# Block 0's second layer as seven products, output weights loaded ahead of batch 1, batch 2 in chunks turned by DMA

## The chip, the cores and the metric

The kernel runs on one core of a Trainium2 chip. A core has TensorE (PE; its weight loads are listed apart as PEld), VectorE (DVE), ScalarE (ACT), GpSimd (POOL), and SyncE (SP), which here does nothing but issue DMAs; 16 DMA engines move the data between HBM and the on-chip SBUF. PE writes its results into PSUM, eight banks of 128 partitions by 2 KB. The metric is the device time of one execution in microseconds (us), as a median of several.

## The reference

A retention layer without softmax over 8 batches of 8 heads, 576 tokens and 64 dimensions, and behind it two dense layers with a tanh GELU over all 4608 tokens:

```python
scores = scale * np.matmul(q, k.transpose(0, 1, 3, 2))
Dmat = np.where(rel >= 0, gamma[:, None, None] ** rel[None, :, :], 0.0)
attn = np.matmul(scores * Dmat[None, :, :, :], v)
x = np.ascontiguousarray(attn.transpose(0, 2, 1, 3)).reshape(B * S, H * D)   # 4608 x 512
h = x @ w_in                                                                 # 512 x 2048
g = 0.5 * h * (1.0 + np.tanh(c * (h + 0.044715 * h * h * h)))
return g @ w_out                                                             # 2048 x 512
```

All inputs and the output are float32. The decay factors over into a factor for each query row and one for each key row, so that only a triangular mask is left within a chunk of 128 tokens, and a running state of 64 x 64 for each head carries the past from chunk to chunk.

## The kernel before

**Blocks.** The dense layers run in nine blocks `t` of 512 tokens (`TB`). Blocks 0 to 7 hold the first 512 tokens of batch 0 to 7, block 8 the last 64 tokens (the tails) of all eight. The attention of batch `b = t + 1` is woven into block `t`, so block `t + 1` finds its input `xT`. A block's first layer is 16 column groups of `w_in` (`up`, L466, 4 matmuls of 512 columns each; `up_half`, L482, two groups for 256 tokens at a time in blocks 0 and 1), each followed by a GELU on ACT into `gT`. The last two blocks run part of the first layer as Strassen-like products.

**Second layer.** Blocks 1 to 8 run it as seven products in place of eight (`prod`, L651, a variant of Strassen's method with halves of the tokens, of the 2048 inner columns and of the 512 output columns). Each product `m` has two token halves `u` of 8 matmuls with 256 columns. It needs four sums of activations (`act_sums`, L637, DVE, into `gs`, one of them in place) and four of weights (`weight_sums`, L626, DVE, into `wt`); `after` (L673) collects the products on DVE and ACT into an output tile `ost` and stores it. Block 0 instead multiplies plainly: `down_mm` (L605), 64 matmuls of 512 columns over 16 rows-of-128 of `w_out` in the order `FO`, the first 12 for two pairs of token tiles, then the 4 late ones; `store_pair` (L610) copies and stores.

**Loads.** All of q, k, v and the weights go through 16 slots of 256 KB (`ld`), and every load is issued by SP from one list `seq` (L124), in order; a slot comes free when its cast to float16 is issued, and `pump` (L136) then issues the next load. Before: batch 0, `w_in`, 12 rows of `w_out`, half of batch 1, 4 rows of `w_out`, the rest of batch 1, batch 2, batch 3, the tails of batches 0 and 1 (`load_tails`, L81, own tiles `lt`), batch 4 and so on. In `load` (L91) batches below `NPE` (3) come in a pair layout, two neighbouring tokens to a partition, in runs of 512 bytes; later batches in 128-token chunks, in runs of 256 bytes.

**Attention.** In the pair layout keys and queries are cast and scaled on POOL or DVE (`cast`, L247), turned by PE (`turn`, L277, 8 transposes of 128 x 128, then one copy of 128 x 1024 on ACT) and used by `score2`, `masks2`, `state2`, `av2`. From batch `NPE` on they are turned by two DMA transposes on SP's queue (`turn_dma`, L296; its third, `ett`, turns the tails) and used by `score`, `masks`, `state`, `av`. `scan` (DVE) and `spread` (ACT) move the state on, `past` multiplies by it, `put` (ACT) writes `xT`.

**Order.** All is written by hand: `at(t, u, f)` puts work after step `u` of block `t`, negative steps lying in block 0's first layer. Engines run their own instructions in this order. For batch 3 and later the casts stand in block `b - 2` from step 16 on (L945 to L957): there the list of loads is put on hold, POOL waits on a small `gate` copy for the block's last activation sums, the transposes follow the last cast, and `resume` lets the loads go on at step 29, so that the transposes stand ahead of them in SP's queue. Loads already issued at that time, up to 16 slots, stand ahead of the transposes. The scores of batch `t + 1` come at steps 9 and 19 of block `t`, values at 15 and 25.

Of the kernel before, what the change touches and what calls it, by code (L numbers as in the profile page):

```python
# [20 lines left out]
def kernel(  # L21
# [9 lines left out]
    nc = tc.nc  # L31
# [9 lines left out]
    NH = NF // 2  # L41
    W = NC * 512
    NB = W // 128
    NPE = 3
    LD = 16
    TB = 512
    NI = TB // 128
# [13 lines left out]
    def bank(name, dt=F32):  # L61
        n = spare.popleft()
        t = ps.tile([128, 512 if dt == F32 else 1024], dt, tag=f"p{n}", name=name, bufs=1)
        home[id(t)] = (n, t)
        return t
# [53 lines left out]
    def body(b):  # L119
        if b < NPE:  # L120
            return [("b", b, key, 2 * g + y) for g in range(2) for key in "qkv" for y in range(2)]
        return [("b", b, key, c) for c in range(NC) for key in "kqv"]

    seq = body(0) + [("i", g, ct) for g in range(4) for ct in range(4)]  # L124
    FO = [f + g for f in (0, 4) for g in (0, 1, 2, 3, 8, 9, 10, 11)]
    LATE = 12
    seq += [("o", f) for f in FO[:LATE]]
    TP = {2: 0, 4: 2, 6: 4, 7: 6}
    seq += body(1)[:6] + [("o", f) for f in FO[LATE:]] + body(1)[6:]
    for b in range(1, B):  # L130
        seq += body(b) if b > 1 else []
        if b - 1 in TP:
            seq.append(("t", TP[b - 1]))
    q_ld = {"next": 0, "free": LD, "hold": False}

    def pump(freed=0):  # L136
        q_ld["free"] += freed
        while q_ld["next"] < len(seq) and not q_ld["hold"]:
            s = seq[q_ld["next"]]
            if s[0] != "t":  # L140
                if q_ld["free"] == 0:
                    return
                q_ld["free"] -= 1
            q_ld["next"] += 1
            {"b": load, "i": load_w_in, "o": load_w_out, "t": load_tails}[s[0]](*s[1:])
# [456 lines left out]
    def ost():  # L602
        return sb.tile([128, 2, DM], F32, tag="ost", name="ost", bufs=2)

    def down_mm(t, i, f):  # L605
        if f == FO[0]:
            op[i] = bank("op")
        nc.tensor.matmul(op[i], gT[t][:, f, i], w_out_sb[:, f, :], start=(f == FO[0]), stop=(f == FO[-1]))

    def store_pair(t, i0, eng):  # L610
        o = ost()
        for n in range(2):
            x = op.pop(i0 + n)
            eng[n](out=o[:, n], in_=x)
            drop(x)
        r0 = TB * t + 128 * i0
        nc.sync.dma_start(out=out[r0 : r0 + 256, :].rearrange("(n p) d -> p n d", n=2), in_=o)

    HD = DM // 2
    wt = {n: const.tile([128, NH, HD], F16, name="wt" + n) for n in "1234"}
    W11, W12 = w_out_sb[:, 0:NH, 0:HD], w_out_sb[:, 0:NH, HD:DM]
# [24 lines left out]
        if 1 in parts:  # L648
            nc.vector.tensor_tensor(out=s["4"], in0=a12, in1=s["2"], op=ALU.subtract)  # L649

    def prod(t, m, u):  # L651
        g = gT[t].rearrange("p f (u i) n -> p f u i n", i=2)
        lhs = {
            1: lambda f: g[:, f, u, 0], 2: lambda f: g[:, NH + f, u, 0], 3: lambda f: gs[t]["4"][:, f, u],
            4: lambda f: g[:, NH + f, u, 1], 5: lambda f: gs[t]["1"][:, f, u], 6: lambda f: gs[t]["2"][:, f, u],
            7: lambda f: g[:, f, u, 1],
        }[m]
        rhs = {1: W11, 2: W21, 3: W22, 4: wt["4"], 5: wt["1"], 6: wt["2"], 7: wt["3"]}[m]
        tag = {1: "A", 2: "A", 3: "C", 4: "D" if t in WIN else "B", 5: "C", 6: "B", 7: "B"}[m]
        if t in WIN and m == 3:  # L660
            tag = "EF"[u if t == NTB - 1 else 0]
        new = tag not in op
        if new:
            op[tag] = bank("op" + tag)
        for f in range(NH):
            nc.tensor.matmul(  # L666
                op[tag][:, HD * u : HD * u + HD], lhs(f), rhs[:, f],
                start=(new and f == 0), stop=(f == NH - 1), skip_group_check=True,
            )
# [3 lines left out]
    def after(t, m, u):  # L673
# [15 lines left out]
        def end(o, i, v, d=slice(0, DM)):  # L689
            b = 4 * v + 2 * i  # L690
            for h, e in enumerate((nc.sync, nc.scalar)):
                r0 = S * (b + h) + M0
                e.dma_start(out=out[r0 : r0 + TL, d], in_=o[TL * h : TL * h + TL, d])
        if m == 1:
            keep["s1"] = sb.tile([128, 2, HD], F32, tag="k1", name="k1", bufs=1)
            nc.scalar.copy(out=keep["s1"], in_=pr("A"))  # L696
# [39 lines left out]
    def cast_w(kind, *i):  # L736
        src = w_raw.pop((kind,) + i)
        if kind == "i":
            g, ct = i
            dst = w_in_sb[:, ct, 512 * g : 512 * g + 512]  # L740
        else:
            dst = w_out_sb[:, i[0], :]
        eng = WENG[kind][CP[kind] % len(WENG[kind])] if CP[kind] < LATE or kind == "i" else nc.gpsimd.tensor_copy
        CP[kind] += 1
        eng(out=dst, in_=src)  # L745
        pump(1)

    WENG = {
        "i": (nc.gpsimd.tensor_copy,),
        "o": (nc.gpsimd.tensor_copy, nc.vector.tensor_copy),  # L750
    }

    def cc(b, key, c, eng):
        cast(b, key, c, eng)
# [45 lines left out]
    for x in range(2):  # L800
        masks2(0, 1, x)
        if x == 0:
            later(0, 2)
    for g in range(4):
        for ct in range(4):
            cast_w("i", g, ct)
    up_half(0, 0, 0)
# [24 lines left out]


    at(0, -12, lambda: [V.memset(x, 0.0) for x in (tbd[1][:, 1:], *tbt[1:])])
    for n, f in enumerate(FO):
        at(0, -5 + n // 4 if n < LATE else 6, lambda f=f: cast_w("o", f))
        if 8 <= n < LATE:
            at(0, -5 + n // 4, lambda n=n: weight_sums(0, [n - 8], V))

    def group(b, g, turns, s, o, own=True, ahead=(), apart=0, late=None):  # L840
        for w, key in zip(turns, "qk"):
# [26 lines left out]
        if own:  # L868
            at(*(late or (o[0], o[1] + 1)), lambda: spread(b, 2 * g + 1, A.copy))

    def casts2(b, g, kq, v, e):
        at(*kq, lambda: [cc(b, key, 2 * g + y, P) for key in "qk" for y in range(2)])
        at(*v, lambda: [cc(b, "v", 2 * g + y, e) for y in range(2)])

    at(0, -1, lambda: (new_casts(1), new_turned(1)))
    casts2(1, 0, (0, 2), (0, 18), A)
    group(1, 0, ((0, 13), (0, 17)), (0, 20), (0, 29), apart=4, late=(1, 1))
    casts2(1, 1, (0, 14), (0, 15), P)
    group(1, 1, ((0, 31), (1, 0)), (1, 1), (1, 5), late=(1, 6))
    at(1, 0, lambda: (new_casts(2), new_turned(2)))  # L880
    casts2(2, 0, (1, 0), (1, 0), P)
    group(2, 0, ((1, 4), (1, 6)), (1, 10), (1, 15), ahead=((2, 1),))
    casts2(2, 1, (1, 4), (1, 4), P)
    at(1, 9, lambda: weight_sums(4, (1, 2), V))
    at(1, 12, lambda: weight_sums(4, (0, 3), V))
    at(1, 16, lambda: later(2, 2))
    at(1, 23, lambda: later(2, 3))
    group(2, 1, ((1, 9), (1, 12)), (1, 20), (1, 26), own=False)
    at(1, 14, chunk_masks)

    at(6, 0, lambda: load_tails(TP[7]))
    at(6, 18, lambda: cast_tails(TP[7]))
# [30 lines left out]
        for w in work:  # L923
            put(*w)

    nb = NPE
    at(1, 26, lambda: state(nb, 0, 1))
    for c in range(2):
        at(2, c, lambda c=c: later(nb, c))
    for t in range(2, B):  # L930
        b, tl = t + 1, TP.get(t)
        s0, o0, s1, o1 = 9, 15, 19, 25
        at(t, s0, lambda t=t, tl=tl: scores(t, 0, tl))
        at(t, o0, lambda t=t, b=b, tl=tl: outs(t, 0, tl, (b, 2, 3) if t < B - 1 else None))
        if b == B:
            continue
        at(t, s1, lambda t=t, b=b: scores(t, 2))
        at(t, o0 + 1, lambda b=b: later(b, 2))
        at(t, o1, lambda t=t, nb=b + 1: outs(t, 2, None, (nb, 0, 1) if nb < B else None))
        at(t, o1 + 1, lambda b=b: later(b, 3))  # L940
        if b + 1 < B:
            for c in range(2):
                at(t + 1, c, lambda c=c, nb=b + 1: later(nb, c))

    for b in range(NPE, B):  # L945
        ent = [(key, c) for c in range(NC) for key in "kqv"]
        eng = {"k": P, "q": P, "v": P if b == NPE else A}
        t0, ut = b - 2, [16, 16, 17, 18, 18, 19, 20, 20, 21, 22, 22, 23]
        if b == NPE:
            ut = [16, 16, 17, 19, 19, 20, 22, 22, 23, 25, 25, 26]  # L950
        at(t0, ut[0], lambda b=b: (new_casts(b), new_turned(b)))
        at(t0, ut[0], lambda: q_ld.update(hold=True))
        at(t0, ut[0], lambda t=t0: nc.gpsimd.tensor_copy(out=gate, in_=gs[t]["4"][:, NH - 1, 1, 0:1]))  # L953
        for u, (key, c) in zip(ut, ent):
            at(t0, u, lambda b=b, key=key, c=c, e=eng[key]: cc(b, key, c, e))
        at(t0, ut[-1] + 1, lambda b=b: turn_dma(b, TP.get(b - 1)))
        at(t0, 29, resume)  # L957

    order = [(u, g) for u, g in ((0, 0), (0, 1), (1, 0), (1, 1), (0, 2), (1, 2), (0, 3), (1, 3))]
    for n, (u, f) in enumerate([(u, f) for u, g in order for f in (4 * g, 4 * g + 2)]):  # L960
        if n > 1:
            up_half(0, u, f)
# [2 lines left out]
    for t in range(NTB):  # L965
        steps = []
        if t == 0:
            for i0, fs in ((0, FO[:LATE]), (2, FO[:LATE]), (0, FO[LATE:]), (2, FO[LATE:])):
                for f in fs:
                    steps.append(lambda f=f, i0=i0: [down_mm(0, i0 + n, f) for n in range(2)] and None)  # L970
                if fs[-1] == FO[-1]:
                    steps.append(lambda i0=i0: store_pair(0, i0, (V.tensor_copy if i0 else A.copy, V.tensor_copy)))
        else:
            for u in range(2 if t == 1 else 0):
                for f in (0, NH, 2, NH + 2, 4, NH + 4, 6, NH + 6):
# [81 lines left out]
```

## Time and profile before

| | before |
|---|---|
| time, median of 3 runs | 296.76 us (296.52 to 296.77) |
| profiled execution: time | 296.39 us |
| profiled execution: span, first to last instruction | 294.7 us |
| PE busy | 282.2 us, 96% of the span |
| DVE, ACT, POOL busy | 191.7, 168.4, 100.2 us |
| bytes read from HBM, written | 36.70 MB, 9.44 MB |
| DMA packets under 512 B, of all | 101632 of 129058 |
| PE at work on block 0's second layer, first and last matmul | 33.6 to 51.9 us |
| block 1, first and last matmul | 51.9 to 87.1 us |
| block 2's first matmul | 87.1 us |

The profiler draws one execution. The page has a row for each engine in 40 slices of the span (a digit is the busy share in tenths), groups of instructions by line of the kernel, and waits: the idle time of an engine just before an instruction, with what ended it. A matmul's own duration overlaps its neighbours, so a stream is priced by the distance between starts. A DMA has a time of issue on SP's queue and a time to landing. A busy DMA row says that packets were under way in all 16 engines; how much they moved is in the GB/s row.

### The profile page before, as it was taken

How to read it: one execution, taken by the hardware profiler on the slowest of the kernel's cores; microseconds unless marked ns; L12 is line 12 of the kernel's file. 1: busy time of each engine (PE TensorE's matmuls, PEld its weight loads, DVE VectorE, ACT ScalarE, POOL GpSimd, SP SyncE). 2: the span in 40 equal slices, each digit the busy share in tenths (PEclk: the TensorE clock that was granted, in tenths of full speed). 3: DMA queues.
4: the chain of work that ended last, by engine and by line, in shares of the span. 5: the costliest groups of instructions: out<-in, count | busy, mean ns of one | idle time of the engine just before them, and what ended most of it. 6: DMA issues, size and time to landing. Idle time of an engine off the chain costs nothing. (4 is left out here: it accounts for less than half of the span.)

```text
span 294.7 us, 7531 instructions
## 1 busy us (share of the span) xinstructions
PE 282.2 (96%) x3100; PEld 204.3 (69%) x3100; DVE 191.7 (65%) x396; ACT 168.4 (57%) x313; POOL 100.2 (34%) x133
## 2 busy tenths in 40 slices
PE   6779999999999999999999999999999999999993
PEld 2458745888884588448844885478547887887782
DVE  6790606789754873477448654855488968974863
ACT  5377443998239663866386736664666258507800
POOL 4587487960880082007700640059030000000000
PEclk9999999999999999999999999999999999999998
DMA  7999999999969998999899949944941030003013
GB/s 202 307 357 372 341 317 292 280 280 211 194 165 232 216 225 169 261 214 194 103 271 221 169 88 273 211 109 76 263 93 38 0 145 1 2 20 125 1 38 107
DMA packets 129058, 52.92 MB, mean 180 GB/s; under 512 B 101632, under 2 KB 120576, under 8 KB 129024
## 3 DMA queue, kind: packets, MB, share of 16 engines
q1 hardware_dynamic: 128544, 51.92, 74.5%
q8 instruction: 24, 0.39, 0.6%
q10 hardware_dynamic: 480, 0.52, 0.6%
q14 instruction: 10, 0.08, 0.1%
HBM read 36.70 MB, written 9.44 MB: 157 GB/s over the span
## 5 line engine op out<-in xcount | busy, mean ns | idle before, releaser
L471 PE MATMUL hp<-xT,w_in_sb 128*128 128x512 f16 x352 | 79.0, 379 | 0.0
L477 ACT ACTIVATE gT<-hp 128x512 f16<-128x512 f32 x88 | 50.6, 597 | 31.0 <-PE hp L471 30.4
L471 PEld LDWEIGHTS <-w_in_sb 128*128 128x128 f16 x352 | 34.0, 98 | 38.2
L666 PEld LDWEIGHTS <-gT 128*128 128x128 f16 x512 | 49.0, 98 | 7.2 <-issue 0.5
L666 PEld LDWEIGHTS <-s 128*128 128x128 f16 x384 | 37.1, 98 | 4.8
L645 DVE TENSOR_TENSOR s<-gT 128x512 f16<-128x512 f16 x32 | 14.4, 449 | 28.0 <-ACT gT L477 27.0
L953 POOL COPY gate<-s 128x1 f16<-128x1 f16 x5 | 0.9, 190 | 90.7 <-DVE s L649 90.7
L489 PE MATMUL hp<-xT,w_in_sb 128*128 128x256 f16 x256 | 30.3, 273 | 1.1 <-POOL w_in_sb L745 0.9
L666 PE MATMUL opA<-w_out_sb,gT 128*128 128x256 f16 x256 | 31.0, 273 | 0.1
L425 ACT CAST tbd<-ws 64x256 f16<-64x256 f32 x48 | 19.4, 405 | 16.0 <-DVE ws L416 15.4
L489 PEld LDWEIGHTS <-w_in_sb 128*128 128x128 f16 x256 | 24.5, 98 | 4.9 <-POOL w_in_sb L745 1.6
L666 PE MATMUL opB<-wt,gT 128*128 128x256 f16 x224 | 26.9, 273 | 0.1
L383 DVE TENSOR_TENSOR ret<-st,cm 128x512 f16<-128x512 f32 x40 | 24.8, 681 | 0.0
L266 POOL TENSOR_TENSOR cq<-ld,sc 128x512 f16<-128x512 f32 x20 | 21.7, 1086 | 0.0
L460 ACT CAST xT<-xs 128x512 f16<-128x512 f32 x36 | 19.3, 592 | 3.3 <-PE xs L450 1.8
L266 POOL TENSOR_TENSOR ck<-ld,sc 128x512 f16<-128x512 f32 x20 | 21.0, 1050 | 0.0
L495 ACT ACTIVATE gT<-hp 128x512 f16<-128x512 f32 x32 | 18.5, 602 | 3.8 <-PE hp L489 3.5
L680 DVE TENSOR_TENSOR k<-k,opB 128x512 f32<-128x512 f32 x16 | 11.0, 687 | 14.2 <-ACT k L696 7.5
L711 ACT COPY ost<-opA 128x512 f32<-128x512 f32 x8 | 4.7, 586 | 24.1 <-PE opA L666 17.5
L293 ACT COPY tt<-tr 128x1024 f16<-128x1024 f16 (+1 forms) x12 | 11.8, 998 | 10.8 <-PE tr L287 10.7
L416 DVE TENSOR_TENSOR ws<-vs,gt 128x256 f32<-128x256 f32 x24 | 15.7, 654 | 1.1
L666 PE MATMUL opC<-wt,s 128*128 128x256 f16 x128 | 15.5, 273 | 0.0
(124 smaller groups left out, 440.0 us busy)
## 6 DMA issues: line engine op xcount, KB each, us to landing
ld<-in_q_dram SPq DMA_DIRECT2D x32, 256.0 KB, 5.3
ld<-in_k_dram SPq DMA_DIRECT2D x32, 256.0 KB, 5.3
ld<-in_v_dram SPq DMA_DIRECT2D x32, 256.0 KB, 5.4
out_dram<-ost SPq DMA_DIRECT2D x16, 512.0 KB, 3.8
ld<-in_moe_w_in_dram SPq DMA_DIRECT2D x16, 256.0 KB, 5.9
ld<-in_moe_w_out_dram SPq DMA_DIRECT2D x16, 256.0 KB, 5.3
lt<-in_k_dram SPq DMA_DIRECT2D x8, 128.0 KB, 5.4
lt<-in_q_dram SPq DMA_DIRECT2D x8, 128.0 KB, 4.3
```

Source lines behind the costliest of these rows:

```text
L266: eng.tensor_tensor(out=dst.rearrange("p (h d) -> p h d", d=D), in0=raw.rearrange("p (h d) -> p h d", d=D), in1=sc[:, s0].unsqueeze(2).to_ ...
L293: cp(out=o, in_=t)
L383: nc.vector.tensor_tensor(out=r.rearrange("p (n i) -> p n i", i=128), in0=t.rearrange("p (n i) -> p n i", i=128), in1=(cm if b < PAIR else ...
L416: nc.vector.tensor_tensor(out=w, in0=uc, in1=gt, op=ALU.mult)
L425: cp(out=(tbd[b % 2][r, c, :, r] if c < NC - 1 else tbt[b % NT4][r, :, r]), in_=w[r])
L460: nc.scalar.copy(out=xT[:, g0 : g0 + 2], in_=xs.rearrange("p (n g t) -> p g n t", n=HP, g=2))
L471: nc.tensor.matmul(hp.rearrange("p (g t) -> p g t", t=TL), w_in_sb[:, ct, 128 * fc : 128 * fc + 128], xT[:, o : o + TB // TL, ct, :], star ...
L477: nc.scalar.activation(out=gT[t][:, fc].rearrange("p i n -> p (i n)"), in_=hp, func=AF.Gelu_apprx_tanh)
L489: nc.tensor.matmul(hp[:, 256 * x : 256 * x + 256].rearrange("p (g t) -> p g t", t=TL), w_in_sb[:, ct, 128 * (f + x) : 128 * (f + x) + 128] ...
L495: nc.scalar.activation(out=gT[t][:, f : f + 2, 2 * u : 2 * u + 2, :].rearrange("p f i n -> p f (i n)"), in_=hp.rearrange("p (f n) -> p f n ...
L645: nc.vector.tensor_tensor(out=s["1"], in0=a21, in1=a22, op=ALU.add)
L666: nc.tensor.matmul(op[tag][:, HD * u : HD * u + HD], lhs(f), rhs[:, f], start=(new and f == 0), stop=(f == NH - 1), skip_group_check=True,)
```

## The change

Five things change together.

1. Block 0's second layer runs through `prod` and `after` like the others, in the order 1, 5, 2, 3, 6, 7, 4, with PSUM tags and collecting sums of its own; products 2 and 6 (`HALF`) run in two halves of the inner columns. It has 14 steps of 8 or 16 matmuls. Its `act_sums` stand in block 0's first layer, and the `weight_sums`, which stood partly in block 1, stand in block 0. `down_mm` and `store_pair` go.
2. All 16 rows of `w_out` are loaded ahead of batch 1. Their casts go to POOL, three (`BY_ACT`) to ACT; none is left on DVE.
3. The first layer's column groups of block 0 are loaded and used in the order 0, 2, 1, 3 (`QS`).
4. `NPE` is 2, so batch 2 is loaded in chunks, cast on POOL (values on ACT) in steps 0 to 10 of block 1, turned by two DMA transposes behind step 10, scored at steps 18 and 24 of block 1, with values at 21 and 28. The list of loads holds behind batch 2 (`"h"`) and resumes at step 12 of block 1 with batch 3, the tails and four loads of batch 4.
5. Times are moved: batch 1's casts and turns in block 0, batch 3's casts (last at step 25, transposes at 26 where they stood at 27), and the first scores and values of block 2 at 11 and 16 where they stood at 9 and 15.

```diff
-    NPE = 3
+    NPE = 2
...
-    seq = body(0) + [("i", g, ct) for g in range(4) for ct in range(4)]
-    FO = [f + g for f in (0, 4) for g in (0, 1, 2, 3, 8, 9, 10, 11)]
-    LATE = 12
-    seq += [("o", f) for f in FO[:LATE]]
+    QS = (0, 2, 1, 3)
+    seq = body(0) + [("i", g, ct) for g in QS for ct in range(4)]
+    seq += [("o", f) for f in range(NF)] + body(1)
     TP = {2: 0, 4: 2, 6: 4, 7: 6}
-    seq += body(1)[:6] + [("o", f) for f in FO[LATE:]] + body(1)[6:]
     for b in range(1, B):
         seq += body(b) if b > 1 else []
+        if b == NPE:
+            seq.append(("h",))
         if b - 1 in TP:
             seq.append(("t", TP[b - 1]))
...
             s = seq[q_ld["next"]]
+            if s[0] == "h":
+                q_ld["hold"] = True
+                q_ld["next"] += 1
+                return
...
-    def prod(t, m, u):
+    def prod(t, m, u, fs=range(NH)):
...
+        if t == 0:
+            tag = "AAEFCBD"[m - 1]
...
-        for f in range(NH):
+        for f in fs:
...
+        if t == 0 and m != 1 and m != 2:
+            if m == 6:
+                for n, a, b in (("u2", "s1", "B"), ("u3", "u2", "C")):
+                    keep[n] = sb.tile([128, 2, HD], F32, tag="k" + n[1], name="k" + n[1], bufs=1)
+                    add(keep[n], keep[a], pr(b))
+                    drop(op.pop(b))
+                add(keep["o0"][:, :, HD:DM], keep["u3"], pr("E"))
+                drop(op.pop("E"))
+                send(keep["o0"], 0)
+            elif m == 7:
+                keep["o1"] = ost()
+                add(keep["o1"][:, :, HD:DM], keep["u3"], pr("D"))
+                add(keep["u2"], keep["u2"], pr("D"))
+                drop(op.pop("D"))
+            elif m == 4:
+                add(keep["o1"][:, :, 0:HD], keep["u2"], pr("F"))
+                drop(op.pop("F"))
+                send(keep["o1"], 1)
+            return
...
+    HALF = (2, 6)
+    BY_ACT = (11, 13, 15)
...
-    for n, f in enumerate(FO):
-        at(0, -5 + n // 4 if n < LATE else 6, lambda f=f: cast_w("o", f))
-        if 8 <= n < LATE:
-            at(0, -5 + n // 4, lambda n=n: weight_sums(0, [n - 8], V))
+    for f in range(NF):
+        at(0, f // 4 - (f == 11) if f in BY_ACT else -7 + f // 2 if f < 8 else -1, lambda f=f: cast_w("o", f))
+    for u, f, ns in ((-4, 0, (0,)), (-1, 4, (0,)), (2, 0, (1,)), (3, 0, (2, 3)), (5, 4, (1, 2)), (6, 4, (3,))):
+        at(0, u, lambda f=f, ns=ns: weight_sums(f, ns, V))
+    for w, f, u in ((-12, 0, 0), (-8, 0, 1), (-2, 4, 0), (-1, 4, 1)):
+        at(0, w, lambda f=f, u=u: act_sums(0, f, f + 4, slice(u, u + 1)))
...
-    casts2(1, 0, (0, 2), (0, 18), A)
-    group(1, 0, ((0, 13), (0, 17)), (0, 20), (0, 29), apart=4, late=(1, 1))
-    casts2(1, 1, (0, 14), (0, 15), P)
-    group(1, 1, ((0, 31), (1, 0)), (1, 1), (1, 5), late=(1, 6))
-    at(1, 0, lambda: (new_casts(2), new_turned(2)))
-    casts2(2, 0, (1, 0), (1, 0), P)
-    group(2, 0, ((1, 4), (1, 6)), (1, 10), (1, 15), ahead=((2, 1),))
-    casts2(2, 1, (1, 4), (1, 4), P)
...
-    group(2, 1, ((1, 9), (1, 12)), (1, 20), (1, 26), own=False)
-    at(1, 14, chunk_masks)
+    casts2(1, 0, (0, 6), (0, 9), A)
+    group(1, 0, ((0, 7), (0, 9)), (0, 10), (0, 12), late=(1, 1))
+    casts2(1, 1, (0, 10), (0, 10), P)
+    group(1, 1, ((0, 13), (1, 0)), (1, 2), (1, 5), late=(1, 6))
+    at(1, 0, chunk_masks)
...
-    for t in range(2, B):
+    U2 = (18, 21, 24, 28)
+    at(1, 16, lambda: state(2, 0, 1))
+    for c in range(2):
+        at(1, 17 + c, lambda c=c: later(2, c))
+    for t in range(1, B):
         b, tl = t + 1, TP.get(t)
-        s0, o0, s1, o1 = 9, 15, 19, 25
+        s0, o0, s1, o1 = U2 if t == 1 else (11 if t == 2 else 9, 16 if t == 2 else 15, 19, 25)
...
-        eng = {"k": P, "q": P, "v": P if b == NPE else A}
-        t0, ut = b - 2, [16, 16, 17, 18, 18, 19, 20, 20, 21, 22, 22, 23]
+        eng = {"k": P, "q": P, "v": P if b == NPE + 1 else A}
+        t0, ut, go = b - 2, [16, 16, 17, 18, 18, 19, 20, 20, 21, 22, 22, 23], 29
+        if b == NPE + 1:
+            ut = [16, 16, 17, 19, 19, 20, 22, 22, 23, 24, 24, 25]
         if b == NPE:
-            ut = [16, 16, 17, 19, 19, 20, 22, 22, 23, 25, 25, 26]
+            t0, ut, go = 1, [0, 0, 1, 3, 3, 4, 6, 6, 7, 9, 9, 10], 12
...
         at(t0, ut[-1] + 1, lambda b=b: turn_dma(b, TP.get(b - 1)))
-        at(t0, 29, resume)
+        at(t0, go, resume)
...
-            for i0, fs in ((0, FO[:LATE]), (2, FO[:LATE]), (0, FO[LATE:]), (2, FO[LATE:])):
-                for f in fs:
-                    steps.append(lambda f=f, i0=i0: [down_mm(0, i0 + n, f) for n in range(2)] and None)
-                if fs[-1] == FO[-1]:
-                    steps.append(lambda i0=i0: store_pair(0, i0, (V.tensor_copy if i0 else A.copy, V.tensor_copy)))
+            for m in (1, 5, 2, 3, 6, 7, 4):
+                for h in range(2):
+                    def part(m=m, h=h):
+                        for u in range(2) if m in HALF else (h,):
+                            prod(0, m, u, range(4 * h, 4 * h + 4) if m in HALF else range(NH))
+                        after(0, m, h)
+                    steps.append(part)
```

## The prediction, made before the changed kernel ran

> **What bounds the kernel now.** I read the page's slices first, then the waits of TensorE (PE), the stretches by window, the time line of PE and that of SyncE's queue (SP).
>
> ```profile
> PE   6779999999999999999999999999999999999993
> PEclk9999999999999999999999999999999999999998
> DMA  7999999999969998999899949944941030003013
> GB/s 202 307 357 372 341 317 292 280 280 211 194 165 232 216 225 169 261 214 194 103 271 221 169 88 273 211 109 76 263 93 38 0 145 1 2 20 125 1 38 107
> ```
>
> PE is full from slice 3 on at an undiminished clock; from 33 us to the end it waits once, for ACT's casts of batch 1's values:
>
> ```profile
> PE us L350 <- ACT cv L253: 0.8, 2, 0.5
> ```
>
> So a PE instruction taken out is worth its own length, unless PE then meets something late. The DMA row is just as full until slice 24, while its GB/s fall: what fills it are smaller packets. The stretches give prices:
>
> ```profile
> 28.00:32.00 4.00, 4.00 (x39) 3.59 (x37) 1.27 (x3) 2.64 (x5) 1.83 (x3) 1.00 1.03 379
> 44.00:47.00 3.00, 2.53 (x56) 1.31 (x55) 1.80 (x4) 1.41 (x4) 2.85 (x3) 1.00 1.17 290
> 58.00:61.50 3.50, 3.50 (x71) 3.12 (x69) 3.36 (x5) 3.42 (x7) 3.50 (x5) 1.00 1.09 218
> 85.00:87.00 2.00, 2.00 (x21) 1.80 (x19) 0.69 (x1) 0.64 (x2) 2.00 (x4) 1.00 0.06 10
> 89.00:95.00 6.00, 6.00 (x29) 2.74 (x28) 1.88 (x6) 5.68 (x12) 0.00 (x0) 1.00 1.11 208
> ```
>
> The last column is GB/s. Weights (rows of 2 KB) move at 379, pair-layout loads (512 B runs) at 290, chunk-layout loads (256 B runs) at 218, DMA transposes at 208. A load of 262,144 B so costs 0.69, 0.90 and about 1.22 us, a transpose of 524,288 B 2.5, a 512 KB store about 1.3 (the DMA view of 86 to 93 us shows one at 374 to 398). The 85 to 87 row is the only real hole in the DMA before 95 us: 1.9 us, where SP waits for VectorE's (DVE) output tile.
>
> The place that decides is the first scores of block 2:
>
> ```profile
> 86.23 0.38 SPq L683 DMA_DIRECT2D out_dram<-ost  x1
> 86.79 3.20 SPq L299 DMA_TRANSPOSE tt<-ck  x1
> 90.08 1.86 SPq L299 DMA_TRANSPOSE tt<-cq  x1
> 92.04 1.81 SPq L243 DMA_TRANSPOSE ett<-e  x1
> ...
> 93.96 0.53 SPq L683 DMA_DIRECT2D out_dram<-ost  x1
> ```
>
> ```profile
> 87.06 8.80 PE L471 MATMUL hp<-xT,w_in_sb 128*128 128x512 f16 x40
> 95.79 0.62 PE L374 MATMUL st<-tt 64*128 64x128 f16 x16
> 96.24 0.39 PE L374 MATMUL st<-ett 64*128 64x128 f16 x8
> 96.56 5.35 PE L471 MATMUL hp<-xT,w_in_sb 128*128 128x512 f16 x24
> ```
>
> The listing of issues gives 4.4 us to landing for that `cq` and 3.7 for `ett`: they land at 94.5 and 95.7, and PE reads them at 95.8 and 96.2. There is 0.5 us of slack behind a DMA queue full since the start.
>
> **PE, removed.** Block 0's second layer: 64 matmuls of 512 columns at 0.216 us (24 of L471 in 96.56 to 101.75) = 13.8; now 112 of 256 columns at 0.110 (16 of opA in 72.46 to 74.22) = 12.3; -1.5. Batch 2's 32 PE transposes: a group of 8 delays its successor by 0.45 (57.74 to 58.19), times four: -1.8. Its scores, states and values as pair tiles take 3.8 by the time line, as chunks 3.5 by block 2's: -0.3. The 0.8 wait goes: batch 1's first values land at 42.5 and 43.4 (38.0 + 5 and 6 x 0.90), ACT casts them by 44.0, the states want them at 44.6. Together -4.4. The new order of the first layer's weight groups permutes equal work and costs nothing; the load order is permuted with it.
>
> **Small waits added in block 0.** The last four output weights land at 35.3 + 4 x 0.69 = 38.0; ACT casts `w_out` row 15 until 38.6, and the second half of product 2 wants it at 38.2: +0.4. Batch 1 lands 0.90 apart from 38.0, so q is cast on POOL (1.05 each) until 41.0 and k until 43.0, where PE wants them at 41.0 and 43.2: nothing. At (0,12) the values wait for the masks, behind three new adds of 0.69 on DVE (43.3 to 45.4, then scan 0.4 and masks 2.5, so 48.3 against 47.9): +0.4. Behind each, PE's whole order waits. The 16 `act_sums` (0.44 each, 7 us) and the moved weight sums fit in DVE's idle 20 to 33 us and between products. Bounds for all of this: 0 to 2 us; I take 0.9.
>
> **POOL and ACT, moved.** POOL casts 13 of the output weights (0.63 each, within the 0.69 between landings) where it cast 10; behind them stand batch 1's keys and queries, already counted. Batch 2's values go from POOL to ACT (4 x 0.62), which loses 4 copies of 1.17 out of the PE transposes: less work, but a wait. The last value lands near 65 while ACT comes to its cast at step 10 of block 1, near 62; behind it stand the GELUs. PE goes on into free PSUM banks, 0.88 us a step, so 3 us want four of the eight banks, and no scores hold any then: nothing. Without that cover it were up to 2 us, hidden again by what follows.
>
> **SP and the DMA, moved and added.** Batch 2's 12 loads become chunk loads: 12 x (1.22 - 0.90) = +3.8. Two transposes are new: +4.9. They stand in SP's queue ahead of batch 3's 12 loads, three pairs of tail loads and four loads of batch 4, and batch 3's transposes stand behind all of these. Block 1's store of `o1` falls behind them: -1.3. The 1.9 us hole closes, as SP has the transposes to issue by then. PE's 4.4 us do not help, for the DMA was full and is never fed by PE before this. So `ett` lands at 95.7 + 3.8 + 4.9 - 1.3 - 1.9 = 101.2 instead of 95.7. Counted forward from 38.0: batch 1 10.8, batch 2 14.6, two stores 2.6, transposes 4.9 (landed at 71), batch 3 14.6, tails 3.7, batch 4's four 4.9, three transposes 6.2, which gives 100.3.
>
> First effect: batch 2's scores at (1,18) want `tt` near 70, it lands at 71: 1 us, absorbed below. Second: block 2's scores move two steps later, which is 8 matmuls or 1.75 us of cover. PE would reach them at 95.8 - 4.4 + 0.9 + 1.0 + 1.75 = 95.0; `tt` lands at 99.9. Queued behind the wait is all of PE. The tail scores start at 101.2 where the same work stood at 96.24 + 1.75 = 98.0. **Sum: +3.2 us**, all PE gains lost under the wait. After it DMA has room (slices 19 and 23 are at 4 to 9 tenths; batch 4's transposes land at 118.5 before, its scores start past 126), so the 3.2 stays to the end.
>
> The span becomes 297.9; the profiled execution took 296.39, so 299.6 (it is 0.4 below the median of the runs shown, no more than runs differ). Bounds: a chunk load at 0.90 (packet size free) puts it at 295.8, one at 1.26 (208 GB/s) at 300.1; a new hole as long as the old one adds 1.9. I take 1.22, as the 218 row is the same kind of load.
>
> A rule against the row: the Trainium skill, DMA: Bandwidth & Descriptors, Latency and other measured facts, gives DMA transposes 261 GB/s effective. The trace has 208. By that figure of the Trainium skill the two new ones would cost an estimated 4.0 and not 4.9, and the time would be 298.7; the row decides.
>
> **Rivals.** (1) *The DMA keeps up*: not slower. It decides if batch 3's transposed tiles land before PE comes, 95.0, six microseconds less DMA than I count. For it: packets of 256 B need not queue if other rings run ahead, the DMA share is a mean over 16 engines. Against: issue-to-landing times of 5.3 us and the 218 GB/s row mean a standing queue. Then PE's sum holds: -4.4 + 0.9 + 0 to 1 = 292.9 to 293.9. (2) *Half of it*: chunk loads near 1.0, `ett` near 98: 296.4, no change. (3) *The clock falls in the wait*: PE idles some 5 us at (2,11), longer than any wait of this trace (2.3), and the granted clock drops for as long a stretch afterwards; 4 us of matmuls at half rate add up to 2: 301.6. Against: the clock column is full even beside the 2.3 us wait. The Trainium skill, TensorE: Matmul & The Clock Gate, Part 1, has this rule: an idle window of 3.4 us halves the clock until a busy one has passed, an estimated +1.7; no run here shows it yet. (4) *The products don't shorten block 0*, because weights come late: PE's gain shrinks, but the wait above hides that too: still 299.6.
>
> **Numbers.** Forecast 0.50 with its own range 298.0 to 301.5 (with rival 4 in it), clock rival 0.13, later waits on top 0.07, no change 0.07, DMA keeps up 0.23. A measurement here can tell 0.2%, 0.6 us. Faster 0.23, same 0.07, slower 0.70. The range goes from 293.5, which leaves out about half of rival 1, to 301.8.
>
> **What would show it.** Right: a PE wait of 3 us or more for L374 on `tt` or `ett` in block 2 near 95 to 101; batch 2's loads about 1.2 us apart; the DMA row without the hole at 86; the first layer of block 2 starting 2 to 4 us earlier than 87. Wrong: no such wait, `ett` landed before 97, and a span under 294; or waits of several microseconds in block 0 or 1 that outlast the DMA.

## The result, and the profile after

The changed kernel takes 304.64 us (median of 4, 303.40 to 304.69); the kernel before took 296.64 on the same chip (4 runs, 296.31 to 296.77). The ratio is 1.0244 [1.0207, 1.0280]: 8.0 us slower, where 2.8 were forecast. The profiled execution took 303.40 with a span of 301.7, 7.0 more than the profiled one of before, and the sums below are made against these two.

The slices of the changed kernel:

```profile
PE   6779969999998499999999999999999999999993
PEclk9999999999999699999999999999999999999999
DMA  7999999999999999999799949991972030003013
GB/s 202 311 364 373 362 292 223 239 225 184 204 207 201 250 230 208 252 221 199 137 220 242 201 86 254 223 158 25 193 203 37 2 139 3 0 4 138 2 35 104
```

The 13th and 14th slices of the PE row (90.5 to 105.6 us) are at 8 and 4 tenths, and the clock row has a dent in the second of them. The sixth (37.7 to 45.3 us, in block 0's second layer) is at 6. The DMA row has lost its 6, the hole at 86 us: packets are under way without a break until 143 us. The GB/s fall to 223 in the seventh slice, three slices before they had fallen so far in the kernel before, since batch 2 now comes in short rows. PE's waits from 24 us to the end, in us in all, times, longest:

```profile
PE st L378 <- DMA tt<-cq: 4.7, 1, 4.7
PE opB L656 <- DVE wt L621: 2.0, 1, 2.0
PE tr L291 <- POOL cq L262: 0.6, 1, 0.6
PE st L327 <- DVE ost L670: 0.4, 1, 0.4
PE hp L493 <- ACT gT L499: 0.4, 1, 0.4
```

Where one kind of wait stood, 0.8 us in all, there are now 8.1 us in these lines alone. The largest is the one that the prediction named: the first scores of block 2, on batch 3's queries, turned by DMA. PE's time line there (start, length of the group, and in brackets the idle time before its first instruction), and what SP issued (start and time on the queue):

```profile
86.53 10.52 PE L475 MATMUL hp<-xT,w_in_sb 128*128 128x512 f16 x48
101.80 1.04 PE L378 MATMUL st<-tt 64*128 64x128 f16 x16 [4.75 <-DMA tt<-cq]
102.87 0.61 PE L378 MATMUL st<-ett 64*128 64x128 f16 x8
103.42 5.12 PE L475 MATMUL hp<-xT,w_in_sb 128*128 128x512 f16 x16
108.37 1.04 PE L656 MATMUL opA<-w_out_sb,gT 128*128 128x256 f16 x8
```

```profile
66.55 1.36 SPq L303 DMA_TRANSPOSE tt<-cq  x1
...
93.88 3.28 SPq L303 DMA_TRANSPOSE tt<-ck  x1
97.25 1.98 SPq L303 DMA_TRANSPOSE tt<-cq  x1
99.32 1.69 SPq L247 DMA_TRANSPOSE ett<-e  x1
```

PE comes at 97.05; the queries issued at 97.25 need 4.4 us and land at 101.7, the tails at 102.8, and PE reads them at 101.80 and 102.87. The groups are also longer than they were: the 16 scores take 1.04 us instead of 0.62, and the 16 matmuls of the first layer 4.95 (103.42 to 108.37) instead of 3.46. The stretches show why; the columns are us, busy us and instructions of PE, PEld, DVE, ACT and POOL, then the granted clock, the DMA share and GB/s:

```profile
97.00:101.70 4.70, 0.05 (x1) 0.00 (x0) 0.36 (x2) 0.72 (x2) 0.00 (x0) 0.78 1.11 218
101.70:106.50 4.80, 4.66 (x32) 2.30 (x33) 4.05 (x8) 0.60 (x1) 0.00 (x0) 0.50 1.05 288
106.50:112.00 5.50, 5.50 (x81) 4.14 (x80) 3.60 (x9) 3.37 (x7) 1.11 (x2) 1.00 1.37 225
```

The DMA is full while PE stands still, and the tiles had long been ready to be turned: POOL's last cast of batch 3's queries ends at 87.46, but batch 4's first four loads, issued from 88.49 to 93.77, stand ahead of the transposes on SP's queue. So this wait is for the queue. The clock goes to half during the wait and stays there 4.8 us into the work.

Against the time of before, with two steps' shift of these scores (1.75 us), the tail scores begin 102.87 - 96.24 - 1.75 = 4.9 us late. The half clock adds 1.5 in the 16 matmuls and 0.2 in the tail scores (0.55 instead of 0.32 to the next start), 1.7 to 1.8 together. By block 3's first matmul (124.24, 117.61 before) 6.6 of the 7.0 us are there; the remaining 0.4 is spread over the later blocks.

### The profile page after: what moved, and what is told of

The parts are those of the page before. It is cut to its first block, busy times and chain, and to the rows that moved or that the text cites. A ratio compares the mean times of both kernels' runs of the same rounds, so it can differ in the third digit from the quotient of the medians.

```text
span 301.7 us, 7381 instructions
## 1 busy us (share of the span) xinstructions
PE 281.8 (93%) x3020; PEld 208.1 (69%) x3020; DVE 203.1 (67%) x409; ACT 167.9 (56%) x317; POOL 104.1 (35%) x132
## 5 line engine op out<-in xcount | busy, mean ns | idle before, releaser
L656 PEld LDWEIGHTS <-gT 128*128 128x128 f16 x576 | 55.0, 98 | 8.3 <-issue 0.3
L656 PEld LDWEIGHTS <-s 128*128 128x128 f16 x432 | 41.7, 98 | 7.5 <-issue 2.1
L633 DVE TENSOR_TENSOR s<-gT 128x512 f16<-128x512 f16 x36 | 16.3, 452 | 35.6 <-ACT gT L481 28.0
L656 PE MATMUL opA<-w_out_sb,gT 128*128 128x256 f16 x288 | 35.4, 273 | 0.1
L387 DVE TENSOR_TENSOR ret<-st,cm 128x512 f16<-128x512 f32 x48 | 29.7, 680 | 5.1 <-PE st L378 5.1
L270 POOL TENSOR_TENSOR ck<-ld,sc 128x512 f16<-128x512 f32 x24 | 25.3, 1056 | 6.2 <-DMA ld<-in_k_dram 5.0
L270 POOL TENSOR_TENSOR cq<-ld,sc 128x512 f16<-128x512 f32 x24 | 25.9, 1080 | 3.1 <-DMA ld<-in_q_dram 2.6
L656 PE MATMUL opB<-wt,s 128*128 128x256 f16 x144 | 17.5, 273 | 2.0 <-DVE wt L621 2.0
L634 DVE TENSOR_TENSOR s<-s,gT 128x512 f16<-128x512 f16 x36 | 16.9, 469 | 1.2
L635 DVE TENSOR_TENSOR gT<-gT 128x512 f16<-128x512 f16 x36 | 17.5, 487 | 0.0
```

Of the source, the lines that this page charges most:

```text
L270: eng.tensor_tensor(out=dst.rearrange("p (h d) -> p h d", d=D), in0=raw.rearrange("p (h d) -> p h d", d=D), in1=sc[:, s0].unsqueeze(2).to_ ...
L387: nc.vector.tensor_tensor(out=r.rearrange("p (n i) -> p n i", i=128), in0=t.rearrange("p (n i) -> p n i", i=128), in1=(cm if b < PAIR else ...
L634: nc.vector.tensor_tensor(out=s["2"], in0=s["1"], in1=a11, op=ALU.subtract)
L635: nc.vector.tensor_tensor(out=a21, in0=a11, in1=a21, op=ALU.subtract)
L656: nc.tensor.matmul(op[tag][:, HD * u : HD * u + HD], lhs(f), rhs[:, f], start=(new and f == 0), stop=(f == NH - 1), skip_group_check=True,)
```

## The experiments

**Theory:** the time of block 2's scores is set by what stands ahead of batch 3's transposes in the DMA queue, and the wait then brings down the clock; everything that PE gains or loses before it is swallowed. **Rival:** the new waits in block 0 (the products, their sums on DVE) or the new scores of batch 2 cost the time. Edits are shown against the changed kernel unless another kernel is named. Times are set beside runs of the kernel before on the same chip, whose medians lay between 296.68 and 296.78.

**e1_b4_late.** Batch 4's first four loads go behind batch 3's transposes.

```diff
+        if b == NPE + 1:
+            seq.append(("h",))
```

> Batch 4's first four loads are issued behind batch 3's transposes instead of ahead of them. Theory (DMA queue at block 2's scores, then the halved clock): batch 3's turned queries land 4.0 us earlier, near 97.7 against 101.66, the tails' near 98.9 against 102.83; PE's wait there falls from 4.75 to under 1.5 us, the clock stays at 1.00, and with the 2.3 us that the halved clock costs the time falls by some 6 us, to about 298.5. Rival (the loss is made by the waits in block 0, 3.4 us by the waits view): PE's wait is not what sets the time, and it stays above 302.

Measured: 297.71 (10 runs, 295.90 to 299.91), 1.0028 [0.9994, 1.0062]. Moving four loads gives back nearly all. The waits of this kernel:

```profile
PE hp L477 <- ACT xT L466: 1.9, 1, 1.9
...
PE st L380 <- DMA tt<-cq: 0.6, 1, 0.6
PE st L380 <- DMA ett<-e: 0.4, 1, 0.4
```

The queries land at 97.6 and the tails at 98.8, within 0.1 us of what was expected; 4.75 us of waiting become 1.0, and the clock there is 1.00. A new wait of 1.9 us for ACT opens block 3, whose input was late. The profiled execution was one of the longer ones, 299.56; against that of the changed kernel it is 3.8 us shorter, in the main 3.7 of waiting and 1.7 of clock less the new 1.9. The medians differ by 6.9; what makes other executions shorter still, no trace shows.

**e2_warm.** PE gets 22 matmuls whose result nobody reads, ahead of block 2's first scores.

```diff
+    def keep_warm(n):
+        t = bank("fill")
+        for _ in range(n):
+            nc.tensor.matmul(t, ident, w_in_sb[:, 0, 0:512], start=True, stop=True)
+        drop(t)
...
+        if t == 2:
+            at(t, s0, lambda: keep_warm(22))
```

> 22 matmuls of 512 columns (4.75 us at full clock) that nobody reads stand on PE ahead of block 2's first scores, so PE works where it waited 4.75 us; nothing else is changed. If the halved clock after the wait is a cost of its own: the clock stays at 1.00 through 98 to 107 us and the time falls by 2 to 2.5 us, to about 302.3. If the clock only follows the wait and costs nothing: 304.6, no change. If PE was not free there: more than 306.

Measured: 301.92 (4 runs, 300.13 to 303.50), 1.0171 [1.0125, 1.0216], near the 302.3 that a cost of the clock was to give. The clock is 1.00 from 98 to 108 us, and the 16 matmuls behind the scores take 3.46 us. The profiled execution is the longest of the four, and in it the tiles land over 1 us later than in the changed kernel's (the tails at 104.2), so its time can't be set beside that one; r_warm below runs it again.

**e3_tails_late.** Besides e1's edit, one pair of tail loads leaves the stretch ahead of batch 3's transposes.

```diff
-    TP = {2: 0, 4: 2, 6: 4, 7: 6}
+    TP = {3: 0, 4: 2, 6: 4, 7: 6}
```

> As the run with batch 4's loads behind, and the first pair of tails is loaded, scored and used in block 3 instead of block 2, so six more loads (4.9 us) and the tails' transpose leave the queue ahead of block 2's scores. Theory: batch 3's turned queries land near 93, before PE comes at 97, no wait is left in block 2; the time is then PE's own sum: block 2 starts at 86.5 against 87.1 before, so about 0.5 below the kernel before, 296 (295.5 to 297). Rival (block 0's waits set the time): above 302. A third possibility: the delayed loads make a new wait in block 3, then 297 to 300.

Measured: 298.08, 1.0042 [1.0012, 1.0072], no better than e1. Batch 3's queries land at 92.34, and PE does not wait for them at all; but the third possibility named there came true, one block on:

```profile
124.78 0.62 PE L380 MATMUL st<-tt 64*128 64x128 f16 x16 [0.86 <-DMA tt<-cq]
125.92 0.40 PE L380 MATMUL st<-ett 64*128 64x128 f16 x8 [0.52 <-DMA ett<-e]
```

The loads that were pushed back, and the tails' third transpose, now stand ahead of batch 4's.

**e4_few_sums.** Five of block 0's eight groups of weight sums are left out and set to zero.

```diff
+    at(0, -12, lambda: [V.memset(x, 0.0) for x in (wt["2"][:, 0:4], wt["4"][:, 0:4], *(wt[n][:, 4:8] for n in "234"))])
...
-    for u, f, ns in ((-4, 0, (0,)), (-1, 4, (0,)), (2, 0, (1,)), (3, 0, (2, 3)), (5, 4, (1, 2)), (6, 4, (3,))):
+    for u, f, ns in ((-4, 0, (0,)), (-1, 4, (0,)), (2, 0, (1,))):
```

> Five of the eight weight sums on DVE in block 0 are left out (their tiles hold zeros), 7.1 us of DVE time; products 4, 6 and 7 are computed with wrong weights. PE's wait of 2.0 us in block 0 goes, and most of the other waits there. Theory (block 2's wait for the DMA absorbs all that PE gains before it): the wait in block 2 grows by what is gained, to 6.5 to 8 us, and the time stays within 1 us of 304.6. Rival (block 0's waits cost their length): 2 to 3 us less, 302.

Measured: 302.24 (302.22 to 304.83), 1.0212 [1.0164, 1.0261]: its median is 2.4 us under the changed kernel's, outside what the theory allowed and at the 302 of the rival (the two intervals overlap, 1.0207 to 1.0261).

```profile
PE st L378 <- DMA tt<-cq: 6.9, 2, 5.7
```

Block 2 begins 1.6 us earlier (84.92), yet its scores only 0.6 (101.19): the wait there grows from 4.75 to 5.7, less than the 6.5 to 8 expected. (The other 1.2 of the 6.9 is at batch 2's scores in block 1.) The half clock begins earlier too (97.6 instead of 99.66), so that 3.2 us of it fell on matmuls and not 4.7. By this reading e4's gain is for the greater part clock, and at most 0.6 of it comes from block 0. In e9 the clock is taken out.

**r_after, r_warm, e9_few_warm**, beside each other: the changed kernel and e2's again, and e4's sums left out with 28 unread matmuls.

> The changed kernel itself, beside the next three on one chip. Expected 304.6 again, with single runs between 302 and 305: the stretch at half clock comes in pieces of 3.4 us (6.8 in the profile) that begin at another point of the wait in each run, so what of it falls on matmuls differs.

> The run with 22 matmuls in place of the wait, again. If the halved clock is a cost of its own, it stays 2 to 3 us below the changed kernel of this same call, near 302.

> The five weight sums left out (products 4, 6 and 7 with wrong weights) and 28 matmuls (6.0 us) in place of the longer wait, so that the clock cannot differ. Theory (what PE gains ahead of block 2 is lost in the wait for the DMA): within 0.7 us of the run with 22 matmuls and all sums. Rival (block 0's waits cost their length): 1.5 to 2.5 us below it. The earlier run without the sums was 2.4 us faster than the changed kernel, in its profile 1.2; by the theory that was the clock's phase and 0.6 us of earlier landing.

Measured: r_after 303.26 (299.51 to 304.33), 1.0179 [1.0125, 1.0233], 1.3 under what was expected; r_warm 301.50, 1.0144 [1.0113, 1.0175]; e9 301.36, 1.0143 [1.0110, 1.0176]. PE of r_warm, then of e9:

```profile
97.48 4.91 PE L238 MATMUL fill<-w_in_sb,ident 128*128 128x512 f16 x22
102.32 0.62 PE L384 MATMUL st<-tt 64*128 64x128 f16 x16
102.78 0.39 PE L384 MATMUL st<-ett 64*128 64x128 f16 x8
```

```profile
96.48 6.21 PE L238 MATMUL fill<-w_in_sb,ident 128*128 128x512 f16 x28
102.62 0.62 PE L384 MATMUL st<-tt 64*128 64x128 f16 x16
103.08 0.39 PE L384 MATMUL st<-ett 64*128 64x128 f16 x8
```

In r_warm the scores come no earlier, but at full clock, and the 16 matmuls behind take 3.47 us. The medians of r_after and r_warm differ by 1.8 us, but their intervals overlap, so the size rests on the traces, and there it differs by execution: 1.7 in the changed kernel's profile, 0.9 in r_after's (4.18 us for the 16 matmuls and 0.2 in the tail scores), where half clock lasted 3.4 us and not 6.8.

With the clock out of it, e9 is 0.14 us under r_warm, although block 2 then starts at 86.12 and not at 87.12. That alone does not show that block 0's loss is swallowed, for in neither run does PE wait for the tiles: they land at 99.8 and 101.2 in r_warm, at 101.7 and 102.9 in e9, and the unread matmuls, 1.3 us more of them in e9, end after the first of these. What shows it is where the tail tile lands: at 102.8 in the changed kernel, 102.9 in e9 and 102.2 in e4, whether block 2 begins at 86.53, 86.12 or 84.92. Of 1.6 us gained ahead of block 2, e4 brings 0.6 to the scores, and even these may be chance, as with the same order of loads the tail tile landed anywhere from 101.2 (r_warm) to 104.2 (e2). So the rival that block 0's waits cost their whole length falls by the traces; a part of it, up to these 0.6, stands.

**e5_products.** The first three points of the change alone; batch 2 stays in pairs.

```diff
-    NPE = 2
+    NPE = 3
```

(and with it the old calls that cast, turn and use batch 2 in blocks 0 to 2)

> The part on block 0 alone: seven products, all output weights loaded ahead of batch 1, batch 1's new times; batch 2 again in pair layout, turned by PE, with the times of the kernel before. Theory: no wait for the DMA in block 2 and the clock at 1.00, as the queue is as long as before; block 1 starts about 1.1 us later than before, as it does in the changed kernel (52.98 against 51.85), because 3.4 us of waits in block 0 outweigh 1.5 us of matmuls and 0.8 us of wait removed; time 297.9 (297 to 298.7). Rival (the products are what makes the changed kernel slow): above 302.

Measured: 297.98, 1.0036 [1.0013, 1.0060]. The products alone cost 1.2 us, as expected here. There is the wait of 1.96 us on `wt` again, and 0.3 for the tails. The profiled execution (298.99) has half clock from 45.6 to 49.0, right behind the 1.96; how much of the 1.2 is clock was not tested.

**e6_chunks.** The other part alone: the kernel before with batch 2 turned by DMA, batch 4's and 5's loads held back behind the transposes, tails as in e3, block 2's scores at step 9. The main lines, against the kernel before (the rest moves batch 2's work as in the change):

```diff
-    NPE = 3
+    NPE = 2
...
-    TP = {2: 0, 4: 2, 6: 4, 7: 6}
+    TP = {3: 0, 4: 2, 6: 4, 7: 6}
...
+        if b in (NPE + 1, NPE + 2):
+            seq.append(("h",))
```

> The part on batch 2 alone, on the kernel before: block 0 with plain matmuls and the old order of loads, batch 2 in chunks turned by DMA in block 1; with the queue relieved (first tails in block 3, batch 4's and batch 5's first four loads behind the transposes ahead of them), block 2's scores at the old step 9. Theory: PE saves 2.1 us of batch 2's work in block 1, loses up to 1 us waiting for batch 2's transposes in block 1, and meets no other wait: 295.6 (295 to 296.7). If the longer queue cannot be relieved by order alone, a wait of over 2 us stays in block 2 or 3: 298 or more.

Measured: 296.34, 0.9983 [0.9959, 1.0007]: no wait for `tt`. The time is inside the range that was given (295 to 296.7), but the interval holds 1, so at most a small gain is shown where 1.1 was expected. Its profiled execution (296.74) had a stretch of half clock at 19.2 to 22.6, ahead of every difference from the kernel before; whether that explains the rest was not tested.

**e7_holds.** The changed kernel with the order of loads of e6.

> The changed kernel with the first tails in block 3 and both holds (batch 4's and batch 5's first four loads behind the transposes). Against the run with the tails late its wait of 0.9 and 0.5 us at block 3's scores goes: its profiled span falls from 294.9 to about 293.5, the time to 295.2 if that profile is typical. If the later loads starve ACT's casts of values instead, a wait on xT at block 3's or 4's start takes its place and the time stays at 296.5 to 298.

Measured: 297.44, 1.0017 [0.9993, 1.0040]: a miss, 2.2 us over what was expected. No wait for `tt` is left. What is left is the `wt` wait, and in the profiled execution what follows it:

```profile
44.23 1.03 PE L658 MATMUL opB<-wt,s 128*128 128x256 f16 x8 [1.96 <-DVE wt L623]
```

```profile
43.10:45.00 1.90, 0.77 (x8) 0.68 (x8) 1.87 (x2) 0.63 (x2) 1.90 (x2) 1.00 1.17 290
45.50:48.90 3.40, 3.40 (x77) 2.45 (x75) 2.85 (x6) 1.25 (x2) 3.40 (x4) 0.50 1.26 238
48.90:52.00 3.10, 3.10 (x61) 2.68 (x58) 3.07 (x6) 0.93 (x3) 2.82 (x8) 1.00 0.92 192
```

PE is full in the second stretch and still gets half the clock, 3.4 us long. In the changed kernel's profile the same wait of 1.96 us was followed by full clock. So block 0's wait can cost here, where the large wait no longer swallows it. Its length differs: in the profiles of e1, e2 and e3 the same `wt` wait is 0.5. There PE had waited 0.6 us for POOL's cast of an output weight just before, and in e1 and e3 three of DVE's last four activation sums fell into a pause of POOL, against one in the changed kernel.

Why is `wt` late? DVE's groups of the changed kernel between 24 and 47 us (instructions, then busy us and mean ns):

```profile
L621 DVE TENSOR_TENSOR wt<-wt,w_out_sb 128x1024 f16<-128x1024 f16 x2 | 2.8, 1420 | 0.1
L635 DVE TENSOR_TENSOR gT<-gT 128x512 f16<-128x512 f16 x4 | 3.3, 826 | 0.0
L637 DVE TENSOR_TENSOR s<-gT,s 128x512 f16<-128x512 f16 x4 | 3.3, 825 | 0.0
```

The prediction had 0.44 for the activation sums (L635, L637) and no price for the weight sums (L621). The next run tests whether they take so long because POOL casts beside them.

**e8_act_casts.** e7 with two more of the output weights' casts on ACT, so that POOL pauses (edit against e7).

```diff
-    BY_ACT = (11, 13, 15)
+    BY_ACT = (11, 12, 13, 14, 15)
```

> As the run with both holds, and the casts of output weight rows 12 and 14 go from POOL to ACT, so POOL is idle from about 36 to 38.5 us. If DVE's float16 operations are slow because POOL works beside them: the activation sums in that stretch fall from 0.83 to 0.43 us each, DVE is 1.5 us further on, and PE's wait for the weight sums of product 6 falls from 2.0 to about 0.5; the time falls by 0.5 to 1.5 us against the run with both holds. If they are slow for another reason, the sums stay at 0.83 and nothing moves.

Measured: 297.13, 1.0000 [0.9979, 1.0022], 0.3 under e7 with intervals that overlap, so the gain of 0.5 to 1.5 us is not shown. What DVE does is plain, however:

```profile
35.20 0.83 DVE L635 TENSOR_TENSOR s<-gT 128x512 f16<-128x512 f16 x1
36.06 0.42 DVE L636 TENSOR_TENSOR s<-s,gT 128x512 f16<-128x512 f16 x1
...
38.52 0.69 DVE L623 TENSOR_TENSOR wt<-w_out_sb,wt 128x1024 f16<-128x1024 f16 x1
39.13 1.53 DVE L623 TENSOR_TENSOR wt<-w_out_sb 128x1024 f16<-128x1024 f16 x1
40.70 1.42 DVE L623 TENSOR_TENSOR wt<-wt,w_out_sb 128x1024 f16<-128x1024 f16 x1
```

POOL has nothing to do from 35.8 to 38.9 us, and then goes on casting:

```profile
27.68 8.07 POOL L758 CAST w_out_sb<-ld 128x512 f16<-128x512 f32 x10
38.88 2.69 POOL L264 TENSOR_TENSOR cq<-ld,sc 128x512 f16<-128x512 f32 x2 [3.14 <-DMA ld<-in_q_dram]
```

In the pause the sums take 0.42 and 0.69; beside POOL's plain casts ahead of it 0.70 to 0.83 and 1.09, beside its scaled casts behind it 1.42 to 1.53 for the larger ones. The `wt` wait is gone and block 1 starts at 51.00 (52.98 in the changed kernel). But PE waits 0.54 us for `tt` in block 1 and 1.92 in block 4 (half clock from 158.0 to 161.4). I took this for batch 5's transposes standing behind loads too; the next run tests it.

**e10_three_holds.** e8 with the loads held back behind one more batch's transposes (edit against e8).

```diff
-        if b in (NPE + 1, NPE + 2):
+        if NPE < b < 6:
```

> As the run with both holds and ACT's casts, with batch 6's first four loads behind batch 5's transposes too. Theory: the wait of 1.9 us at block 4's scores goes (batch 5's turned tiles land 4 to 5 us earlier), and with it that run's stretch at half clock at 158 us; 295.5 (294.8 to 296.5), below the kernel before. If the later loads of values hold up ACT in block 4 or 5: 297 or more.

Measured: 296.05, 0.9964 [0.9936, 0.9991], inside the range that was given, 7.2 us under r_after on the same chip and slightly under the kernel before. Its longest waits from 24 us on:

```profile
PE tr L293 <- POOL ck L264: 0.5, 1, 0.5
PE hp L495 <- ACT gT L501: 0.4, 1, 0.4
PE st L380 <- DMA tt<-cq: 0.4, 1, 0.4
```

Nothing over 0.5 us is left. So it was the placement of loads, tails and two casts, and not the work itself, that made the change lose. What the work gains is less than was forecast, however: from block 0's second layer to the last group of matmuls PE needs 253.3 us (34.30 to 287.61) against 255.3 before (33.56 to 288.84), 2.0 us and not 3.5 (4.4 less 0.9), with 1.8 us of small waits in it.

## Why the prediction was right, and where it was wrong

**Right: place, cause, sign.** The wait of 4.75 us is at L378 in block 2, on `tt` and then `ett`; I had PE at 95.0 and `tt` at 99.9, a wait of 4.9; that the lengths agree so well is luck, as PE (97.05) and the queries (101.7) were both about 2 us late. It is the queue: e1 takes four loads out of it and 4.75 becomes 1.0. The DMA row without its hole came as named. That PE's own gains would be lost in the wait is borne out for the greater part by e4 (1.6 us earlier in block 2, 0.6 at the scores).

Of the 3.8 us between the forecast of 299.6 and the profiled execution's 303.40, 1.7 are transposes that landed later than the sum had it, 1.7 to 1.8 the clock, which the sum put at nothing, and 0.4 lies in later blocks.

**Wrong: the clock (rival 3).** This step failed in kind. I kept the clock full because it was "full even beside the 2.3 us wait". That wait is `fill`'s at the very start, ahead of the first matmuls, and says nothing about a wait in mid-stream. The clock stood at half for 6.8 us, 4.7 of them on matmuls: +1.7 to 1.8, and none of it in e2 and r_warm, where PE was kept at work. The rule in the Trainium skill, TensorE: Matmul & The Clock Gate, Part 1, put beside the rival as +1.7, agrees with this in size, but by luck: it was reckoned with one window of 3.4 us at half clock, all of it on matmuls, where here there were two, 2.1 us of them in the wait. At 0.13 the rival was too low: the sum already held a wait of nearly 5 us, so it belonged in the forecast, 299.6 + 1.8 = 301.4.

**Wrong in size: the DMA sum, 1.6 us short.** `ett` landed at 102.8, and not at 101.2. Taken by landings: batch 1's last load at 48.4 (48.8 forecast), batch 2's loads and two stores 18.0 us (`o1` at 66.4, 66.0 by the count) instead of 17.2, so the 1.22 us for a chunk load was nearly right. The pair of transposes took 6.0 us (`o1` to 72.4) instead of 4.9, batch 3's loads 15.8 instead of 14.6, the tails 4.9 instead of 3.7, batch 4's four 4.0 instead of 4.9, and the last three transposes 5.8 instead of 6.2. The forward count had 100.3, the backward one 101.2; what was lacking lies in the new transposes, batch 3's loads and the tails, each of which I had priced by a stretch of its own kind. Why they took longer here was not tested.

**Wrong, and for the greater part hidden here: small waits in block 0.** I had 0.9, bounds 0 to 2; PE waited 3.0 us in block 0's second layer (1.96, 0.6, 0.4) and began 0.3 later, so that layer took 19.2 us, and not less than the 18.3 of before; another 0.4 of waiting follows in block 1. The failed step is that the sums "fit in DVE's idle 20 to 33 us and between products": I took 0.44 for an activation sum, the mean over the whole kernel before, and no price for a weight sum. The trace of before held the warning: in its block 1, at 59 to 63 us and beside POOL's casts, the first activation sums took 0.83 to 1.27 us. PE came to the scores at 97.05, not 95.0, and block 2 began 0.5 us earlier than before, not 2 to 4. The large wait swallowed most of this; in e7, where that wait is gone, it shows.

**Products and chunks apart.** Rival 4 (block 0 is not shortened) was so, though not, in this trace, because weights came late (other profiles have 0.3 to 0.6 us of waits for POOL's cast of one); e5 gives +1.2 us for that part alone. e6 shows that batch 2 in chunks, with the loads held back, costs nothing (-0.4 us, within the noise). Neither sums to +8.0. The chunks alone with the old order of loads were not run; that the order makes the difference rests on e1, e7 and e10.

**Left open.** Why runs of one and the same kernel differ by 3 to 4 us (e7: 295.91 to 298.92). Among them are the changed kernel's first four: the sums above hold for the profiled one, 303.40, the other three took 1.2 to 1.3 us more, and no trace shows where. Further, when 2 us of waiting cost the clock, and the last 0.4 us of the sum.

## What to carry to other kernels

When a queue is full up to a consumer, add up every transfer that stands ahead of the consumer's own, and put what is not wanted yet behind it: four loads moved were worth 7 us in the medians here. A wait of PE in mid-stream costs its length and can bring a stretch at half clock besides (each wait of 4.75 us and more did here), so price both; once it is removed, look for the next batch in the same queue and for the smaller waits that it had hidden. Take an operation's duration from a stretch in which its neighbours are as busy as they will be.

## What the runs showed of the hardware

**The clock falls after short waits, sometimes.** Waits of 4.75 and 4.84 us in block 2 brought half clock both times, which began within the wait and lasted 6.8 us in the one execution and 3.4 (101.9 to 105.3) in the other; one of 5.7 us (e4) brought 6.8. Waits of 1.9 to 2.0 us went either way: about 3.4 us at half clock followed in e5, e7, e8 and r_warm, and full clock in the changed kernel, in r_after and (1.85 us, at block 3) in e1. The Trainium skill, TensorE: Matmul & The Clock Gate, Part 1, names an idle window of about 3.4 us. The length of the pieces agrees with that, but waits well below it were enough in four profiles, and in e6 half clock came at 19.2 us behind 3.4 us in which PE worked for 1.8 and no single wait exceeded 0.62.

Within one execution the changes of the clock lie whole multiples of 3.41 us apart: in r_warm it falls at 8.51, 46.06 and 298.64 us, 11 and 85 such steps after the first, and is back at 11.92 and 49.47. So it matters where a wait lies on this grid. Counted back from the fall at 101.91, a boundary of r_after's grid, 43.89, cuts its wait of 1.96 us (42.85 to 44.81) in two, and the clock stayed full; e7's (42.27 to 44.23) lies within one step, 42.04 to 45.46, and the clock fell at its end. The grid is not the whole of it: the changed kernel's wait (43.12 to 45.08) lies almost wholly within one step too, 41.63 to 45.05, and full clock followed.

**DVE and POOL slow each other down.** Float16 sums of two SBUF operands on DVE take 0.42 us (128 x 512) and 0.69 (128 x 1024) with POOL idle. Beside POOL's casts they take 0.70 to 0.83 and 1.06 to 1.53. POOL's scaled casts of 128 x 512 take 1.43 to 1.47 us beside DVE's sums and 1.04 behind them (two at 38.71 in 2.86 us, and one each at 54.23 and 55.23 in 1.04, in the changed kernel). The Trainium skill, SBUF — State Buffer, section SBUF: two separate sides, has these two engines share a pair of ports, held for a whole instruction while the other waits. The traces agree in that each slows the other; what they show is 1.5 to 2.2 times on DVE's side and 1.4 on POOL's, with both engines at work.
